# Causal attention and a gated MLP on one core: how VectorE adds 1e-9, what the planner takes TensorE to cost, and 66-column weight loads

## The chip, the cores and the metric

The kernel runs on one core of one Trainium2 chip. A core has TensorE (PE; its weight loads are listed as PEld), VectorE (DVE), ScalarE (ACT), GpSimd (POOL) and SyncE (SP), which here issues nearly all DMAs. The metric is the device time of one execution in microseconds (us), smaller is better.

## The reference

There are 4 batches of 12 heads, 448 positions, head size 64. Then comes an MLP on 1792 tokens of width 768 with a hidden width of 1536. All data is float32.

```python
scores = scale * np.matmul(q, k.transpose(0, 1, 3, 2))
scores = np.where(mask, -1000000000.0, scores)          # mask: above the diagonal
scores = scores - np.max(scores, axis=-1, keepdims=True)
attn = np.exp(scores)
attn = attn / (np.sum(attn, axis=-1, keepdims=True) + 1e-09)
x = attn @ v                                             # heads side by side: (1792, 768)
g = x @ w_gate
out = (g * (1 / (1 + np.exp(-g))) * (x @ w_val)) @ w_out
```

## The kernel before, in words

The work goes in four chunks, one for each batch. A *unit* is one head of one batch, 48 in all; numbers in names such as T24_2 or S22 begin with the unit's number. Heads are worked in pairs. While the MLP of chunk c runs on TensorE, the attention of chunk c+1 is mixed into it, a few matmuls at a time.

Precision: an operand of a matmul is split into a rounded high part and a low remainder (`xh`, `xl`; `hh`, `hl`; `ph`, `pl`; both halves of `whl`), and three products high x high, high x low, low x high are added (`mm3`, lines 871 to 876). The weights of the MLP are unpacked and split once, during chunk 0: a `wide` tile is loaded, ACT or POOL writes `top`, DVE builds `wraw` (L857), ACT or POOL rounds it into the high half of `whl` and DVE or POOL subtracts to get the low half (L333 or L336). The split is stored to DRAM, and later chunks load it back.

The attention of a unit, in the order of its stages: `score` (L505, 24 matmuls for a pair of heads, written "S"); `rowmax` (L553, DVE, four blocks: mask, scale, row minimum of the negated scores, an accumulator read behind each); `expo` (L565, ACT, writes the row's sum into `sums`); `recip` (L576 and L577, DVE: add 1e-9, then the reciprocal); normalising `p` (L609 on ACT, L613 on POOL, or DVE); `transp` and `transp0` (L699, L667: transposes of `p` into a bank "T"); an eviction of T into `ph` (ACT L311 or DVE L314), the remainder into `pl` or the low part of `ph` (DVE L333); `pv` (L741, seven matmuls into a bank "O").

From chunk 1 on there is one T bank, so a group of transposes starts only when the `ph` and the `pl` of the group before have been read out of it. A score needs four banks (two tags of two), so the score of the next pair waits for all eight rowmax blocks of the pair before.

`FEW` (line 51) is the number of columns that a weight load takes where 64 would do: the first block of a score (L504) and the `pl` matmuls (L740).

The order of the work is not written by hand: `Planner.run` (line 104) is a list scheduler. Every operation has the engines that could do it, each with a cost in us (`cost`, line 64; for TensorE also `TURN`, line 42, added where the kind of matmul changes: m for the MLP, s score, t transpose, o `pv`, v `pv` of chunk 0), and a due time. The planner picks operation by operation, by these numbers, on which engine and in which place it stands; the engines then run in that order, with semaphores. Its numbers change no instruction, only the order and the engine. `NR` (line 24) is the number of rows of `sums` and `rec` that units take in turn.

Of the kernel before, what the change touches and what calls it, by code (L numbers as in the profile page):

```python
# [8 lines left out]
F32 = mybir.dt.float32  # L9
# [6 lines left out]
ALU = mybir.AluOpType  # L16

P = 128
D = 64
# [1 line left out]
CUTS = [[0, 64, 192, 320, 448], [0, 64, 192, 320, 448], [0, 64, 192, 320, 448], [0, 64, 192, 320, 448]]  # L21
WID = [0, 64, 192, 320, 448]
CHUNKS = [[(0, 0, 448)], [(1, 0, 448)], [(2, 0, 448)], [(3, 0, 448)]]
NR = 8
SLOPE0 = 1.0
WLEAD = 1.2
XD = [-10.0, 3.0]
# [11 lines left out]
SHARED = 0.5  # L39
PVLATE = 0  # L40
LAT = {"PE": 0.29, "DVE": 0.2, "ACT": 0.23, "POOL": 0.2, "SP": 0.1}
TURN = {'ms': 0.19, 'sm': 0.19, 'mt': 0.0, 'tm': 0.0, 'ts': 0.19, 'st': 0.19, 'mv': 0.15, 'vm': 0.15, 'tv': 0.15, 'vt': 0.15, 'sv': 0.15, 'vs': 0.15, 'om': 0.055, 'os': 0.1, 'so': 0.19, 'ot': 0.03}
TS = 0.0
PF = 1.12
GF = 1.25
# [18 lines left out]
def cost(e, kind, n):  # L64
    if e == "ACT":
        return {"psum": 66, "sbuf": 110, "ptr": 190, "exp": 280, "tanh": 160}[kind] / 1e3 + n / 1200
    if e == "DVE":
        return 0.075 + n / {"one": 1920}.get(kind, 960)
    if e == "POOL":
        return {"one": 190, "ptr": 260, "two": 180}[kind] / 1e3 + n / {"two": 465.0}.get(kind, 1200.0)  # L70
    return {"r": max(n * 0.4475e-3 + 0.0025, 0.109), "n": n / 600, "t": n * 0.109 / 128}[kind] + 0.001


class Res:
# [154 lines left out]
def kernel(  # L229
# [8 lines left out]
    nc = tc.nc  # L238
# [5 lines left out]
    NKC = len(CUTS[0]) - 1  # L244
# [5 lines left out]
    cpool = ctx.enter_context(tc.tile_pool(name="cpool", bufs=1))  # L250
# [12 lines left out]
    masks = cpool.tile([P, P + maskX + P], F32, tag="masks", name="masks")  # L263
    back, mask = masks[:, : maskX + P], masks[:, P:]
    both = cpool.tile([P, D], F32, tag="both", name="both")
    all_sums = cpool.tile([P, NR, NKC], F32, tag="sums", name="sums")
    sums = [all_sums[:, i] for i in range(NR)]
    all_rec = cpool.tile([P, NR, NKC], F32, tag="rec", name="rec")
    rec = [all_rec[:, i] for i in range(NR)]
    xs = [cpool.tile([P, T], F32, tag=f"xs{i}", name=f"xs{i}") for i in range(KD)]  # L270
    xh = [cpool.tile([P, T], F32R, tag=f"xh{i}", name=f"xh{i}") for i in range(KD)]
# [9 lines left out]
    cpool.tile([P, 32], F32, tag="pad", name="pad")  # L281
    top = cpool.tile([P, WC], U32, tag="top", name="top")
    nc.vector.memset(top, 0)
    nc.vector.memset(all_sums, 1.0)
    make_identity(nc, ident)
    nc.gpsimd.memset(masks, 0.0)
    for m_, step, base in ((back, 1, 1 - P), (mask, -1, maskX)):
# [10 lines left out]
    def op(alts, due, deps=(), alloc=(), uses=(), extra=0.0):  # L298
        first = [heads[r.tag] for r in alloc if r.tag in heads]
        o = pl_.op(alts, due, list(deps) + first, alloc, uses, extra)  # L300
        o.soft = first
        o.port = bool(alts.pop("port", False))
        o.kb = alts.pop("kb", 0)
        o.kind = alts.pop("kind", "m")
        for r in alloc:
            heads[r.tag] = o
        return o
# [77 lines left out]
    st = [dict() for _ in range(NU)]  # L385
# [6 lines left out]
    def attention(u):  # L392
        U = units[u]
        c, b, h, N, KB = U.c, U.b, U.h, U.n, U.qb
        s = st[u]
# [4 lines left out]
        due = dues[u] = lambda stage: base + (SLOPE if c else SLOPE0) * stage  # L400
# [68 lines left out]
        if h % 2 == 0:  # L469
            if not U.ns:  # L470
                rQ, rK = Res("QS"), Res("KS")
                sp = []
                for nm, r_, src, ld, rr in (("Q", rQ, "q", lq, rq), ("K", rK, "k", lk, rk)):
                    def newsp(nm=nm):
                        s[nm] = buf([P, 2, S], F32R, nm + "S", nm + "S", f"{nm}S{u}")
                        return s[nm][:, 0]
                    x1 = op(copies("sbuf", N, newsp, lambda src=src: s[src + "w"]), due(0), [ld], [r_], [rr])
                    sp.append(op(binary(N, lambda nm=nm: s[nm][:, 1], lambda src=src: s[src + "w"],
                                        lambda nm=nm: raw(s[nm])[:, 0]), due(1), [x1], [], [r_, rr]))
            for gi_, sess in enumerate(FIRST if rest else SG if c == 0 else [sum(SG, [])]):  # L480
                tags = ["S", "X"] if c else ["SXM"[gi_]] if rest else ["MS"[gi_ == 0]]
                rSs = {(y, x): Res(tags[x]) for x in range(len(sess)) for y in (0, 1)}
                steps = sorted(sum(sess, []))

                def score(gi_=gi_, sess=sess, steps=steps, tags=tags):
                    passes = ((None, None),) if U.ns else ((0, 0), (0, 1), (1, 0))
                    for x, blks in enumerate(sess):
                        for y in (0, 1):
                            B_, off = bank(tags[x], f"S{u + y}_{gi_}_{x}"), 0
                            for i in blks:  # L490
                                q1_ = U.qi[i][1][1]
                                st[u + y][f"S{i}"] = B_[:, off : off + q1_]
                                off += q1_
                    for i in steps:
                        q0, q1_ = U.qi[i][1]
                        for z, (a, b_) in enumerate(passes):
                            for y in (0, 1):
                                half = slice(D * y, D * y + D)
                                Q = s["qw"][half] if U.ns else s["Q"][half, a]
                                K = s["kw"][half] if U.ns else s["K"][half, b_]  # L500
                                if U.joint and i == 0:
                                    nc.tensor.matmul(st[u]["S0"][half], Q[:, :D], K[:, :D] if y else K[:, S - D :], start=True, stop=True)
                                    continue
                                r = max(U.rows[i], FEW)  # L504
                                nc.tensor.matmul(st[u + y][f"S{i}"][:r], Q[:, q0 : q0 + r],  # L505
                                                 K[:, :q1_] if y else K[:, S - q1_ :], start=z == 0, stop=z == len(passes) - 1)
                ws = [U.qi[i][1][1] for i in steps]
                if U.ns:
                    so = op({"PE": (sum(cost("PE", "n", w) + 0.06 for w in ws) + TS, score), "kind": "s"}, due(2),
                            (rest if gi_ else some) or [lq, lk], list(rSs.values()), [rq, rk])  # L510
                else:
                    so = op({"PE": (sum(3 * cost("PE", "r", w) for w in ws) + TS, score), "kind": "s"}, due(2), sp,
                            list(rSs.values()), [rQ, rK])
                for x, blks in enumerate(sess):
                    for i in blks:
                        for y in (0, 1):
                            scored[u + y, i] = (so, rSs[y, x])
        for i, (q0, q1_) in U.own:
            r = U.rows[i]
# [17 lines left out]
            so, rS = scored[u, i]  # L537
# [34 lines left out]

        def recip():
            i0, i1 = U.own[0][0], U.own[-1][0] + 1
            sm, rc = sums[u % NR][:, i0:i1], rec[u % NR][:, i0:i1]
            nc.vector.tensor_scalar(rc, sm, 1.0e-9, None, ALU.add)  # L576
            nc.vector.reciprocal(rc, rc)  # L577
        rc = op({"DVE": (0.3, recip)}, due(5), exps, [], [rsum])

# [138 lines left out]
    def weigh(u):  # L718
# [6 lines left out]
        if not npv:  # L725
            rO, dps, use, dur = Res("O"), [], [], 0.0
            for g, o_, w, _, stk, d_, r_ in (blocks[j] for j in range(nj)):
                dps += [x for x in d_ if x not in dps]
                use += [r for r in r_ if r not in use]
                dur += (1 if stk else 2) * cost("PE", "r", w)  # L730

            todo = [(j, "ph") for j in (0, *range(2, nj))] + [(j, "pl") for j in range(nj - 1, 0, -1)] + [(1, "ph")]

            def pv():
                s["O"] = bank("O", f"O{u}")


                for x, (j, t) in enumerate(todo):
                    g, o_, w, _, stk, _, _ = blocks[j]
                    m = FEW if t == "pl" else 2 * D  # L740
                    nc.tensor.matmul(s["O"][:m, U.base(j) - U.qa : N], s["VS"][:, j, :m], s[f"{t}{g}"][:, o_ : o_ + w],  # L741
                                     start=x == 0, stop=x == len(todo) - 1)
            last = op({"PE": (dur, pv), "kind": "o"}, due(10), dps, [rO], use)
            rx, rt = Res(f"xs{h}"), Res("tmp")

            def newt():
                s["tmp"] = buf([D, S], F32, "tmp", "tmp", f"tmp{u}")[:, :N]
                return s["tmp"]
            t1 = op(copies("psum", N, newt, lambda: s["O"][D:P, :N], engines="AD"), due(11), [last], [rt], [rO])
            o = op(binary(N, lambda: xs[k][D * (h % 2) : D * (h % 2) + D, :N], lambda: s["O"][0:D, :N],  # L750
                          lambda: s["tmp"], ALU.add, engines="D"), due(12), [t1] + prevx, [rx], [rO, rt])
            xs_ops.setdefault((c, k), []).append(o)
            xs_res.setdefault((c, k), []).append(rx)
            return
# [261 lines left out]
```

## Time and profile before

| | us |
|---|---|
| median of 3 runs | 683.66 (683.42 to 683.88) |
| the profiled execution | 684.65 |
| its span, first to last instruction | 682.9 |

TensorE's records cover 98% of the span at full granted clock (0.999). The end of a matmul is modelled and matmuls overlap, so what a matmul takes of the stream is read from the start of one to the start of the next. The rows of the profile in the section below are named by their group.

### The profile page before, as it was taken

How to read it: one execution, taken by the hardware profiler on the slowest of the kernel's cores; microseconds unless marked ns; L12 is line 12 of the kernel's file. 1: busy time of each engine (PE TensorE's matmuls, PEld its weight loads, DVE VectorE, ACT ScalarE, POOL GpSimd, SP SyncE). 2: the span in 40 equal slices, each digit the busy share in tenths (PEclk: the TensorE clock that was granted, in tenths of full speed). 3: DMA queues.
4: the chain of work that ended last, by engine and by line, in shares of the span. 5: the costliest groups of instructions: out<-in, count | busy, mean ns of one | idle time of the engine just before them, and what ended most of it. 6: DMA issues, size and time to landing. Idle time of an engine off the chain costs nothing.

```text
span 682.9 us, 10861 instructions
## 1 busy us (share of the span) xinstructions
PE 671.8 (98%) x3898; PEld 598.9 (88%) x3898; DVE 356.7 (52%) x881; ACT 347.8 (51%) x864; POOL 193.7 (28%) x238
## 2 busy tenths in 40 slices
PE   9999999999999999999999999999999999999998
PEld 6567898899888999999999989999999999999997
DVE  5777889898788464355633346545444222222100
ACT  6998688687798363245634336346345211111000
POOL 3766455556162130031322214134232000000000
PEclk9999999999999999999999999999999999999999
DMA  8878899999988865556667665554555675676771
GB/s 293 277 260 308 303 352 390 321 374 314 347 309 324 320 202 201 191 176 215 202 223 239 201 230 189 200 186 139 186 198 164 216 224 213 223 229 212 226 251 41
DMA packets 40118, 165.08 MB, mean 242 GB/s; under 512 B 4480, under 2 KB 13952, under 8 KB 40064
## 3 DMA queue, kind: packets, MB, share of 16 engines
q1 hardware_dynamic: 39904, 164.28, 70.6%
q8 instruction: 31, 0.51, 0.3%
q14 instruction: 23, 0.19, 0.1%
q10 hardware_dynamic: 160, 0.10, 0.1%
HBM read 130.55 MB, written 33.82 MB: 241 GB/s over the span
## 4 chain that ended last, share of the span: by engine, by line
PE 81%; ACT 11%; DVE 6%; issue 1%; POOL 0%; ACTq 0%; DVEq 0%
PE M L874 15%; PE M L875 15%; PE M L876 15%; PE MO L874 8%; PE MO L875 8%; PE MO L876 7%; PE S L505 4%; PE O L741 4%; ACT p L565 4%; PE T L699 3%; ACT p L609 2%; ACT ph L311 1%; ACT top L311 1%; DVE wraw L857 1%; PE T L667 1%
## 5 line engine op out<-in xcount | busy, mean ns | idle before, releaser
L874 PE MATMUL M<-xh,whl 128*128 128x448 f32 x576 | 215.0, 373 | 0.0
L875 PE MATMUL M<-xl,whl 128*128 128x448 f32 x576 | 209.4, 364 | 0.0
L876 PE MATMUL M<-xh,whl 128*128 128x448 f32 x576 | 209.1, 363 | 0.0
L874 PEld LDWEIGHTS M<-xh,whl 128*128 128x128 f32 x576 | 108.2, 188 | 8.5 <-issue 1.7
L876 PEld LDWEIGHTS M<-xh,whl 128*128 128x128 f32 x576 | 108.1, 188 | 7.7
L875 PEld LDWEIGHTS M<-xl,whl 128*128 128x128 f32 x576 | 108.4, 188 | 6.8 <-DVE xl L333 0.3
L874 PE MATMUL MO<-hh,whl 128*128 128x448 f32 x288 | 107.2, 372 | 0.0
L876 PE MATMUL MO<-hh,whl 128*128 128x448 f32 x288 | 104.6, 363 | 0.6 <-DVE whl L333 0.6
L875 PE MATMUL MO<-hl,whl 128*128 128x448 f32 x288 | 104.7, 364 | 0.0
L565 ACT ACTIVATE p<-p,m 128x192 f32<-128x192 f32 (+3 forms) x180 | 91.1, 509 | 3.4 <-DVE m L553 3.3
L311 ACT ACTIVATE ph<-T 128x384 fp32r<-128x384 f32 (+3 forms) x116 | 57.8, 504 | 56.5 <-PE T L667 34.4
L553 DVE CUSTOM_DVE_ANT_0 p<-S,masks 128x192 f32<-128x192 f32 (+3 forms) x180 | 68.3, 426 | 21.4 <-PE S L505 20.2
L311 ACT ACTIVATE hh<-t 128x448 fp32r<-128x448 f32 x40 | 23.1, 577 | 82.0 <-DVE t L917 82.0
L609 ACT ACTIVATE p<-p,rec 128x192 f32<-128x192 f32 (+3 forms) x130 | 58.8, 502 | 9.3 <-DVE rec L577 9.0
L911 DVE SCALAR_TENSOR_TENSOR t<-t,M 128x448 f32<-128x448 f32 x48 | 29.7, 619 | 57.2 <-ACT t L907 56.8
L876 PEld LDWEIGHTS MO<-hh,whl 128*128 128x128 f32 x288 | 54.0, 188 | 4.7 <-DVE whl L333 1.0
L874 PEld LDWEIGHTS MO<-hh,whl 128*128 128x128 f32 x288 | 54.1, 188 | 4.5 <-issue 1.2
L875 PEld LDWEIGHTS MO<-hl,whl 128*128 128x128 f32 x288 | 54.2, 188 | 3.6 <-DVE hl L333 0.3
L917 DVE TENSOR_TENSOR t<-t,M 128x448 f32<-128x448 f32 x48 | 29.6, 618 | 51.0 <-PE M L876 50.6
L907 ACT ACTIVATE t<-M 128x448 f32<-128x448 f32 x48 | 26.0, 542 | 57.5 <-PE M L876 56.9
L333 DVE TENSOR_TENSOR pl<-T,ph 128x384 fp32r<-128x384 f32 x72 | 39.6, 550 | 22.6 <-ACT ph L311 22.3
L699 PE MATMUL T<-ident,p 128*128 128x128 f32 x288 | 46.8, 276 | 3.3 <-DVE pl L333 3.0
(80 smaller groups left out, 822.7 us busy)
## 6 DMA issues: line engine op xcount, KB each, us to landing
whl<-ws SPq DMA_DIRECT2D x108, 768.0 KB, 4.4
wide<-in_w_dram SPq DMA_DIRECT2D x36, 768.0 KB, 6.8
ws<-whl SPq DMA_DIRECT2D x36, 768.0 KB, 7.5
vraw<-in_v_dram SPq DMA_DIRECT2D x24, 256.0 KB, 4.3
out_dram<-osb SPq DMA_DIRECT2D x24, 224.0 KB, 4.7
qraw<-in_q_dram SPq DMA_DIRECT2D x23, 224.0 KB, 4.6
kraw<-in_k_dram SPq DMA_DIRECT2D x23, 224.0 KB, 4.6
qraw<-in_q_dram SPq DMA_DIRECT2D x1, 128.0 KB, 2.5
```

Source lines behind the costliest of these rows:

```text
L311: nc.scalar.activation(out(), in_(), AF.Copy, scale=scale)
L333: r["DVE"] = (cost("DVE", "two", n), lambda: nc.vector.tensor_tensor(out(), a(), b(), alu))
L505: nc.tensor.matmul(st[u + y][f"S{i}"][:r], Q[:, q0 : q0 + r], K[:, :q1_] if y else K[:, S - q1_ :], start=z == 0, stop=z == len(passes) - 1)
L553: nc.vector.tensor_tensor_reduce(p[:r], s[f"S{i}"][:r], mask[:r, maskX - q0 : maskX - q0 + q1_] if h % 2 else back[:r, P - min(q1_, P) : P ...
L565: nc.scalar.activation(p[:r], p[:r], AF.Exp, bias=peak(i)[:r], scale=-1.0, accum_out=sums[u % NR][:r, i : i + 1],)
L609: nc.scalar.activation(p[:r], p[:r], AF.Copy, scale=rec[u % NR][:r, i : i + 1])
L699: nc.tensor.transpose(pt[:, o_ + q0 - bs : o_ + q0 - bs + r], s[f"p{i}"][:r, k0 : k0 + P], ident[:r, :r])
L874: nc.tensor.matmul(out[:, :n], a[:, w], xhi, start=first, stop=False)
L875: nc.tensor.matmul(out[:, :n], a[:, w], xlo, start=False, stop=False)
L876: nc.tensor.matmul(out[:, :n], l[:, w], xhi, start=False, stop=last)
L911: nc.vector.scalar_tensor_tensor(t, t, 1.0, ps[c, f, 0][:, :N], ALU.add, ALU.mult)
L917: nc.vector.tensor_tensor(t, t, ps[c, f, 1][:, :N], ALU.mult)
```

## The change: a sum over pairs, other numbers for the planner, 66 columns

`sums` gets one more row, which is set to 1e-9 once. The first step of `recip` is now a `tensor_reduce` with add over an axis of two: the unit's row and that constant row, reached by a stride. The units take 7 rows in turn instead of 8. The planner's costs change: of turns on TensorE, of a score's 64-wide block (0.062 us a matmul instead of 0.109), and of `pv` (0.001 us more or less a matmul, by width). `FEW` is 66.

```diff
-NR = 8
+NR = 7
...
-TURN = {'ms': 0.19, 'sm': 0.19, 'mt': 0.0, ... 'om': 0.055, 'os': 0.1, 'so': 0.19, 'ot': 0.03}
+TURN = {'ms': 0.15, 'sm': 0.17, 'mt': 0.0, ... 'om': 0.0, 'os': 0.1, 'so': 0.16, 'ot': 0.0}
...
-FEW = 72
+FEW = 66
...
-    return {"r": max(n * 0.4475e-3 + 0.0025, 0.109), "n": n / 600, ...
+    return {"r": max(n * 0.4475e-3 + 0.0025, 0.109), "f": n * 0.4475e-3 + 0.0045, "n": n / 600, ...
...
-    all_sums = cpool.tile([P, NR, NKC], F32, tag="sums", name="sums")
+    all_sums = cpool.tile([P, NR + 1, NKC], F32, tag="sums", name="sums")
...
-    nc.vector.memset(all_sums, 1.0)
+    nc.vector.memset(all_sums[:, :NR], 1.0)
+    nc.vector.memset(all_sums[:, NR], 1.0e-9)
...
-  so = op({"PE": (sum(3 * cost("PE", "r", w) for w in ws) + TS, score), "kind": "s"}, due(2), sp,
+  so = op({"PE": (sum(3 * (0.062 if w == D else cost("PE", "r", w)) for w in ws) + TS, score), "kind": "s"}, due(2), sp,
...
-            sm, rc = sums[u % NR][:, i0:i1], rec[u % NR][:, i0:i1]
-            nc.vector.tensor_scalar(rc, sm, 1.0e-9, None, ALU.add)
+
+            sm, rc = all_sums[:, u % NR :: NR - u % NR, i0:i1], rec[u % NR][:, i0:i1]
+            nc.vector.tensor_reduce(rc, sm.rearrange("p a c -> p c a"), mybir.AxisListType.X, ALU.add)
             nc.vector.reciprocal(rc, rc)
...
-                dur += (1 if stk else 2) * cost("PE", "r", w)
+                dur += (1 if stk else 2) * cost("PE", "f", w)
```

In the changed kernel, lines 285 to 575 stand one lower than before, and later ones two.

Where the order moves, first VectorE behind the first transposes of unit 36 in chunk 2 (rec and sums are shared by all units; T36_1 is a bank of transposes, ph and pl its two evictions). Before:

```order
L577 RECIPROCAL rec_70<-rec_70 128x4
L917 TENSOR_TENSOR t2_0_4627<-t2_0_4627,M2_1_4621 128x448
L314 TENSOR_SCALAR ph36_1_4682<-T36_1_4673 128x384
L576 TENSOR_SCALAR rec_70<-sums_69 128x4
L577 RECIPROCAL rec_70<-rec_70 128x4
L333 TENSOR_TENSOR pl36_1_4690<-T36_1_4673,ph36_1_4682 128x384
L314 TENSOR_SCALAR ph36_2_4706<-T36_2_4697 128x384
```

And the same place now:

```order
L579 RECIPROCAL rec_70<-rec_70 128x4
L919 TENSOR_TENSOR t2_0_4626<-t2_0_4626,M2_1_4622 128x448
L315 TENSOR_SCALAR ph36_1_4683<-T36_1_4674 128x384
L578 TENSOR_REDUCE rec_70<-sums_69 128x4
L579 RECIPROCAL rec_70<-rec_70 128x4
L334 TENSOR_TENSOR pl36_1_4691<-T36_1_4674,ph36_1_4683 128x384
L315 TENSOR_SCALAR ph36_2_4707<-T36_2_4698 128x384
```

Here nothing moved: the reduction stands where the addition stood, between the two evictions.

Second, TensorE at the end of chunk 0, ahead of the score of units 24 and 25 (MO0 is an output bank of the MLP of chunk 0, whl a weight tile, S24 and S25 the score's banks). Before:

```order
L876 MATMUL MO0_3_2560<-hh4_93,whl30_2458 128x448
L874 MATMUL MO0_3_2560<-hh5_94,whl30_2458 128x448
L875 MATMUL MO0_3_2560<-hl5_106,whl30_2458 128x448
L876 MATMUL MO0_3_2560<-hh5_94,whl30_2458 128x448
L699 MATMUL T22_1_2601<-ident_66,p22_1_2529 128x128
L699 MATMUL T22_1_2601<-ident_66,p22_2_2531 128x128
L699 MATMUL T22_1_2601<-ident_66,p22_3_2535 128x128
L505 MATMUL S24_0_0_2606<-KS24_2525,QS24_2523 72x64
L505 MATMUL S25_0_0_2607<-KS24_2525,QS24_2523 72x64
```

And now:

```order
L877 MATMUL MO0_2_2393<-hl11_112,whl29_2441 128x448
L878 MATMUL MO0_2_2393<-hh11_100,whl29_2441 128x448
L743 MATMUL O21_2542<-ph21_0_2419,VS21_2238 128x448
L743 MATMUL O21_2542<-ph21_2_2522,VS21_2238 128x256
L743 MATMUL O21_2542<-ph21_2_2522,VS21_2238 128x128
L743 MATMUL O21_2542<-pl21_2_2533,VS21_2238 66x128
L743 MATMUL O21_2542<-pl21_2_2533,VS21_2238 66x256
L743 MATMUL O21_2542<-pl21_1_2503,VS21_2238 66x384
L743 MATMUL O21_2542<-ph21_1_2491,VS21_2238 128x384
L506 MATMUL S24_0_0_2570<-KS24_2493,QS24_2482 66x64
L506 MATMUL S25_0_0_2571<-KS24_2493,QS24_2482 66x64
```

The score of units 24 and 25 moved ahead of the transposes T22_1 and of 27 matmuls of the MLP: between it and the score of units 22 and 23 there now stand two groups of three transposes, 18 matmuls of the MLP and one `pv`; before there stood one `pv`, 27 matmuls and one group of three.

Third, TensorE where chunk 1's MLP begins (M1_0 is its first bank; T24_2 and T25_0 both use the one T bank). Before:

```order
L874 MATMUL M1_0_3007<-xh5_82,whl36_2838 128x448
L875 MATMUL M1_0_3007<-xl5_88,whl36_2838 128x448
L876 MATMUL M1_0_3007<-xh5_82,whl36_2838 128x448
L699 MATMUL T24_2_3038<-ident_66,p24_2_2668 128x128
L699 MATMUL T24_2_3038<-ident_66,p24_3_2675 128x128 x2
L874 MATMUL M1_1_3046<-xh0_77,whl37_2852 128x448
L875 MATMUL M1_1_3046<-xl0_83,whl37_2852 128x448
```

And now:

```order
L506 MATMUL S29_0_0_2976<-KS28_2832,QS28_2830 128x448
L701 MATMUL T24_2_3008<-ident_66,p24_2_2637 128x128
L701 MATMUL T24_2_3008<-ident_66,p24_3_2649 128x128 x2
L669 MATMUL T25_0_3024<-ident_66,p24_0_2413 128x128
L669 MATMUL T25_0_3024<-ident_66,p24_1_2628 128x128
L669 MATMUL T25_0_3024<-ident_66,p24_2_2637 128x128
L669 MATMUL T25_0_3024<-ident_66,p24_3_2649 128x128
L876 MATMUL M1_0_3029<-xh0_77,whl36_2901 128x448
```

T25_0 now stands right behind T24_2, with no matmul of another kind between; before, 54 matmuls of the MLP stood between them.

## Rows read from the trace of the kernel before

**Rows 1.** Page, part 1: engine, busy us (share of the span) xinstructions.

```profile
PE 671.8 (98%) x3898; PEld 598.9 (88%) x3898; DVE 356.7 (52%) x881; ACT 347.8 (51%) x864; POOL 193.7 (28%) x238
```

**Rows 2.** Waits of PE: line <- what ended them: us in total, times, longest.

```profile
PE T L699 <- DVE pl L333: 3.0, 4, 1.4
PE O L741 <- DVE ph L333: 1.2, 2, 1.0
...
PE MO L876 <- DVE whl L333: 0.6, 1, 0.6
```

**Rows 3.** Line L576: count, ns min/median/max, first and last start us, forms.

```profile
L576 DVE TENSOR_SCALAR rec<-sums x48: 151/170/1625, 9.3 to 527.8; 128x4 f32<-128x4 f32 x42, 128x3 f32<-128x3 f32 x6
```

**Rows 4.** Line L577, same columns.

```profile
L577 DVE RECIPROCAL rec<-rec x48: 175/178/179, 9.5 to 528.0; 128x4 f32<-128x4 f32 x42, 128x3 f32<-128x3 f32 x6
```

**Rows 5.** Timeline of DVE, 394 to 398: start us, us, line, operation [idle before].

```profile
394.65 0.56 DVE L314 TENSOR_SCALAR ph<-T 128x384 fp32r<-128x384 f32 x1 [0.31 <-PE T L699]
395.12 1.14 DVE L576 TENSOR_SCALAR rec<-sums 128x4 f32<-128x4 f32 x1
...
396.39 0.53 DVE L333 TENSOR_TENSOR pl<-T,ph 128x384 fp32r<-128x384 f32 x1
```

**Rows 6.** Timeline of POOL, 394 to 398.

```profile
395.08 1.16 POOL L336 TENSOR_TENSOR hl<-t,hh 128x448 fp32r<-128x448 f32 x1
```

**Rows 7.** Timeline of PE, 394 to 398.

```profile
394.12 0.49 PE L699 MATMUL T<-ident,p 128*128 128x128 f32 x3
394.37 0.45 PE L874 MATMUL M<-xh,whl 128*128 128x448 f32 x1
...
397.06 0.52 PE L699 MATMUL T<-ident,p 128*128 128x128 f32 x3 [0.64 <-DVE pl L333]
```

**Rows 8.** Timeline of PE, at 69.

```profile
69.20 0.52 PE L699 MATMUL T<-ident,p 128*128 128x128 f32 x3 [1.40 <-DVE pl L333]
```

**Rows 9.** Timeline of DVE, at 67.

```profile
66.78 1.62 DVE L576 TENSOR_SCALAR rec<-sums 128x4 f32<-128x4 f32 x1 [0.18 <-ACT p L565]
...
68.53 0.53 DVE L333 TENSOR_TENSOR pl<-T,ph 128x384 fp32r<-128x384 f32 x1
```

**Rows 10.** Timeline of POOL, at 67.

```profile
66.55 1.82 POOL L336 TENSOR_TENSOR whl<-wraw,whl 128x768 fp32r<-128x768 f32 x1
```

**Rows 11.** Lines of PEld, by form: names, shapes xcount | busy us, mean ns.

```profile
L741 PEld LDWEIGHTS O<-pl,VS 128*72 128x72 f32 x108 | 9.8, 144 | 0.0
```

**Rows 12.** Page, part 5: line L874's loads.

```profile
L874 PEld LDWEIGHTS M<-xh,whl 128*128 128x128 f32 x576 | 108.2, 188 | 8.5 <-issue 1.7
```

**Rows 13.** Timeline of PE, 300 to 304: a score amid the MLP.

```profile
300.98 0.36 PE L876 MATMUL M<-xh,whl 128*128 128x448 f32 x1
301.27 1.85 PE L505 MATMUL S<-KS,QS 64*72 64x64 f32 x24
303.05 0.47 PE L874 MATMUL M<-xh,whl 128*128 128x448 f32 x1
303.36 0.37 PE L875 MATMUL M<-xl,whl 128*128 128x448 f32 x1
```

**Rows 14.** Timeline of PE, 186 to 200: scores of units 22 and 24.

```profile
188.36 1.84 PE L505 MATMUL S<-KS,QS 64*72 64x64 f32 x24
...
196.97 1.84 PE L505 MATMUL S<-KS,QS 64*72 64x64 f32 x24
```

**Rows 15.** Timeline of DVE, 109 to 112: four rowmax blocks.

```profile
109.45 0.20 DVE L553 CUSTOM_DVE_ANT_0 p<-S,masks 64x64 f32<-64x64 f32 x1
...
110.83 0.07 DVE L553 DVE_READ_ACCUMULATOR2_ANT m<- 128x1 f32 x1
```

**Rows 16.** Lines of DVE, by form.

```profile
L857 DVE SCALAR_TENSOR_TENSOR wraw<-wide,top 128x768 uint32<-128x768 uint32 x36 | 39.5, 1098 | 6.3 <-ACT top L311 5.9
L333 DVE TENSOR_TENSOR whl<-wraw,whl 128x768 fp32r<-128x768 f32 x28 | 31.6, 1129 | 0.9 <-ACT whl L311 0.9
```

**Rows 17.** Windows: stretch, its us, then busy (x) of PE, PEld, DVE, ACT, POOL.

```profile
55.60:182.00 126.40, 123.95 (x735) 111.59 (x734) 109.47 (x218) 100.56 (x225) 67.63 (x60) 1.00 0.95 339
```

More of the change, by code (lines that the diff above doesn't have):

```diff
@@ L41 @@
 LAT = {"PE": 0.29, "DVE": 0.2, "ACT": 0.23, "POOL": 0.2, "SP": 0.1}
-TURN = {'ms': 0.19, 'sm': 0.19, 'mt': 0.0, 'tm': 0.0, 'ts': 0.19, 'st': 0.19, 'mv': 0.15, 'vm': 0.15, 'tv': 0.15, 'vt': 0.15, 'sv': 0.15, 'vs': 0.15, 'om': 0.055, 'os': 0.1, 'so': 0.19, 'ot': 0.03}
+TURN = {'ms': 0.15, 'sm': 0.17, 'mt': 0.0, 'tm': 0.0, 'ts': 0.15, 'st': 0.17, 'mv': 0.15, 'vm': 0.15, 'tv': 0.15, 'vt': 0.15, 'sv': 0.15, 'vs': 0.15, 'om': 0.0, 'os': 0.1, 'so': 0.16, 'ot': 0.0}
 TS = 0.0
@@ L70, in cost @@
         return {"one": 190, "ptr": 260, "two": 180}[kind] / 1e3 + n / {"two": 465.0}.get(kind, 1200.0)
-    return {"r": max(n * 0.4475e-3 + 0.0025, 0.109), "n": n / 600, "t": n * 0.109 / 128}[kind] + 0.001
+    return {"r": max(n * 0.4475e-3 + 0.0025, 0.109), "f": n * 0.4475e-3 + 0.0045, "n": n / 600, "t": n * 0.109 / 128}[kind] + 0.001
 class Res:
@@ L265 @@
     both = cpool.tile([P, D], F32, tag="both", name="both")
-    all_sums = cpool.tile([P, NR, NKC], F32, tag="sums", name="sums")
+    all_sums = cpool.tile([P, NR + 1, NKC], F32, tag="sums", name="sums")
     sums = [all_sums[:, i] for i in range(NR)]
-    all_rec = cpool.tile([P, NR, NKC], F32, tag="rec", name="rec")
+    all_rec = cpool.tile([P, NR + 1, NKC], F32, tag="rec", name="rec")
     rec = [all_rec[:, i] for i in range(NR)]
```

## Prediction, made before the changed kernel had run

> **What bounds the kernel now.** I read the page first: TensorE is covered for 98% of the span, and no other engine for more than 52% [rows 1]. So the end is set by how long TensorE's stream is and by the holes in it. Next the waits of TensorE alone: only a few microseconds are idle, and nearly all of it is ended by VectorE: 3.0 us where transposes wait for `pl` to be read out of the bank, 1.2 where `pv` waits for the low part of `ph`, 0.6 for a split weight [rows 2]. At full clock the stream itself can shrink only by cheaper turns and loads; everything else that the change can do is to make these holes smaller or larger. A change of 1.4 us (0.2% of 683.66) is about what a measurement can tell from nothing, and all the holes together are some 6 us.
>
> Then I asked what is late behind the holes. At 397.06 TensorE's second group of transposes waits 0.64 us for a `pl` [rows 7]. VectorE's queue ahead of that `pl` holds the 1e-9 addition of another unit: it begins at 395.12 and takes 1.14 us, and the `pl` starts at 396.39 [rows 5]. The addition's median is 0.170 us and its longest 1.625, for the same 4 numbers a partition [rows 3]. At 395.08 GpSimd began a subtraction of 1.16 us [rows 6]: it ends at 396.24, and the addition at 396.26. At 66.78 the same: the addition takes 1.62 us [rows 9], inside a GpSimd subtraction from 66.55 to 68.37 [rows 10], the `pl` starts at 68.53, and TensorE, idle for 1.40 us, starts at 69.20 [rows 8]. So VectorE's addition waits for GpSimd's running instruction to end, and twice that wait reaches TensorE. The reciprocal right behind has never taken more than 0.179 us [rows 4].
>
> By the Trainium skill (SBUF — State Buffer, "Who interferes with whom"), GpSimd shares a port pair with VectorE under an exclusive lock, `tensor_scalar` can need that pair, and `tensor_reduce` on this chip never contends. The trace agrees on the first two, the ends lying 0.02 us apart; no run so far shows the third.
>
> **The change, part by part.** All terms are set against the profiled execution (684.65, its span 682.9) and then moved to the median of the runs, which is 0.99 below it.
>
> *The addition becomes a reduction over pairs.* Still 48, one for each unit, in the same step of the same queue. Its own price: 8 numbers a partition read instead of 4. No row has a small reduction; below stands the shortest addition, 0.151, above it the longest, 1.625 [rows 3]; the nearest is the reciprocal, 0.178, also four results from a strided row and never held up [rows 4]. I take 0.18. If it isn't held by GpSimd, the two waits above end: at unit 36 the order around it is unchanged, so the `pl` comes 1.14 - 0.18 = 0.96 us sooner, and the 0.64 of idle time goes [rows 5, 7]. At 69.20 the hole of 1.40 us goes likewise, for the `pl` comes 1.44 sooner [rows 8, 9]. Together -2.0. Ends: 0 (it is held as before) and -3.0, all of the transposes' wait [rows 2].
>
> The skill has a rule against this: a `tensor_reduce` is the slowest VectorE operation and should be restructured away on a hot path (VectorE: DVE Perf Modes, "Rules for kernel authors"). The reciprocal's row says that at this size the fixed part is nearly all. By that rule the 48 reductions would cost a little more each on an engine that is 52% busy; by the row, nothing. The sum goes by the row.
>
> One more memset, and 7 rows in turn instead of 8 (a unit then waits for the normalisation of the unit 7 before it, long done): nothing.
>
> *66 columns.* A load of 72 columns takes 144 ns [rows 11], one of 128 takes 188 [rows 12]: 0.79 ns a column, 4.7 ns for six. There are 108 such loads in scores and 108 in `pv`. If each is in the way, 216 x 4.7 = 1.0 us; if the matmuls cover them, 0. Only the first block of a score (64 columns a matmul) and the 128-wide matmuls of `pv` are short enough to let a load show, about half: -0.5.
>
> *The order: turns.* From the order, TensorE changes kind 292 times before and 287 times now, and five scores, not two, now lead straight into transposes. A score amid the MLP costs 0.29 us up to its start, and 0.31 from the next matmul to the second, where a step of the MLP is 0.20 [rows 13]; so a turn is worth 0.1 us, and five to three of them -0.3. Ends 0 and -0.6.
>
> *The order: the end of chunk 0.* Here the new order puts work closer to what it waits for. Four places:
>
> (a) T25_0 right behind T24_2 in the one bank. At 394.12 a group of three transposes starts; the eviction starts at 394.65 and takes 0.56 [rows 5], `pl` then 0.53, and from its end to TensorE's start it is 0.14 (68.53 + 0.53 to 69.20) [rows 8, 9]: ready at 395.88, while TensorE went on at 394.37 [rows 7]. What was covered by 54 matmuls is now bare: +1.5.
>
> (b) The score of units 24 and 25. In the order before, the two scores start 8.61 us apart [rows 14]. Nine MLP matmuls fewer (-1.8) and one group of transposes more (+0.3) make 7.1. In that time VectorE must do, from the end of the first score (1.8): eight rowmax blocks (four take 1.45 to the last read's end [rows 15], so 2.9), two evictions of `ph` and two `pl` (2.2 [rows 5]), one `wraw` (1.10 [rows 16]), one reduction and reciprocal (0.36): 8.4, less some overlap and plus whatever it was behind with. I take +1.5, between 0.5 and 2.5.
>
> (c) `pv` of unit 22 six matmuls (1.2 us) behind T23_0, while VectorE has a weight subtraction of 1.13 [rows 16], a 448-wide one and the low part of `ph` in front of it: +1.1, between 0 and 2.
>
> (d) The MLP's first matmuls behind the score wait for a weight subtraction that VectorE does after the rowmax blocks: +0.5, between 0 and 1.
>
> Sum +4.6. In the same stretch the order before had 0.6 (the weight) [rows 2] and, of the 3.0 and the 1.2, what lies behind the holes at 69 and 397: 3.0 - 1.40 - 0.64 = 1.0 and 1.2 - 1.0 = 0.2. Up to 1.5 goes there, so +3.1 net. Ends: +0.5 and +5.
>
> *The order: the rest.* Before, 9 matmuls (1.8 us) stood between two groups of transposes nearly everywhere; now it is 12 at one of two such places. That gives the eviction and `pl` 0.6 us more. But 20 evictions of `ph` moved from ScalarE to VectorE (42 instead of 22 by the order), 0.56 us each [rows 5], 11 us of VectorE work in all. I take -0.8 for chunks 0 to 3 outside the places above, between -1.5 and +2.
>
> DMA: the queue issues the same 280 transfers; none ends a wait of TensorE before [rows 2], so nothing.
>
> Sum: -2.0 - 0.5 - 0.3 + 3.1 - 0.8 = -0.5. 684.65 - 0.5 = 684.15 for such an execution, 683.2 for the median.
>
> **The rivals.**
>
> *Faster: the end of chunk 0 isn't as tight as I count.* VectorE is 109.5 us busy in the 126.4 us from 55.6 to 182 [rows 17]; the held additions are gone, so it may come to the end of the chunk ahead of time, and (b), (c) and (d) shrink to 0.5 in all. (a) and this 0.5 stand against 1.5 of old holes, +0.5: -2.0 - 0.5 - 0.3 + 0.5 - 0.8 = -3.1, that is 680.6. For it speaks that three of four places have a low end near nothing; against it that the work in front of them (weights, rowmax) cannot be put off.
>
> *Slower: VectorE becomes the bound of chunk 0.* It is at 0.87 of that stretch [rows 17]. Roughly half of the 11 us moved onto it falls in chunk 0, +5.5, against some 3 us of held additions that go. If it gets over 0.9, it has no idle time left to catch up after a wait for ScalarE, every late `pl` or low `ph` reaches TensorE, and 2.5 us more are lost: 685.7. It decides from the point where `pl` is late in 55.6 to 182 more often than before.
>
> *The reduction is held by GpSimd just the same.* Then the -2.0 falls out: 685.2. The never-held reciprocal speaks against it.
>
> **How the numbers follow.** The sum, no change that can be told: 0.38, own range 682.3 to 685.0. Faster, about 680.6: 0.35. Slower: VectorE the bound 0.21, the reduction held 0.06, together 0.27. The range that holds 8 in 10 reaches into both rivals, 680.3 to 686.0. Likeliest 683.2.
>
> **What would show it.** Right: the longest reduction is under 0.3 us; at unit 36 the second group of transposes has no idle time before it; in TensorE's waits T25_0 has about 1.5 us, ended by `pl` or by the eviction; the score of units 24 and 25 waits for rowmax; the 66-column loads take about 139 ns. Wrong: reductions as long as a GpSimd instruction; no wait at T25_0; or a total over 686 with TensorE waiting on VectorE throughout 55 to 182 (the order as a whole is then worse, not its end), or under 680 with the end of chunk 0 free of waits.

## The result, and the profile after

The changed kernel took 689.38 us (median of 5, 689.26 to 690.66), the kernel before 683.88 beside it (683.42 to 685.04): 1.0083 times as long, 95% interval 1.0069 to 1.0098. It is slower by 5.5 us, outside the predicted range, and by none of the rivals' mechanisms. The profiled execution took 689.36, its span is 687.6.

The page of the changed kernel, part 1, columns as in [rows 1]:

```profile
PE 675.3 (98%) x3898; PEld 598.0 (87%) x3898; DVE 357.2 (52%) x902; ACT 338.6 (49%) x844; POOL 186.4 (27%) x238
```

TensorE is still covered for 98% of the span, but for 3.5 us more than in [rows 1], with the same 3898 matmuls. So part of the loss lies inside its stream and shows in no wait. The waits of the changed kernel's TensorE, as [rows 2]:

```profile
PE MO L878 <- DVE whl L334: 1.6, 2, 1.3
PE T L669 <- DVE pl L334: 1.3, 1, 1.3
PE T L701 <- DVE pl L334: 1.1, 3, 0.6
PE S L506 <- DVE m L554: 0.9, 1, 0.9
PE T L669 <- POOL p L615: 0.7, 1, 0.7
PE T L701 <- DVE m L554: 0.7, 1, 0.7
```

Of the 3.0 us behind `pl` at the line of the transposes 1.1 are left, and other waits stand beside them: a split weight, the one bare pair of transpose groups (L669 behind `pl` is T25_0), the rowmax blocks (`m`), and once a normalisation of `p` on GpSimd.

The additions of the changed kernel by line (count, ns min/median/max), against [rows 3, 4]:

```profile
L578 DVE TENSOR_REDUCE rec<-sums x48: 140/156/165, 9.4 to 528.5; 128x4 f32<-128x8 f32 x42, 128x3 f32<-128x6 f32 x6
L579 DVE RECIPROCAL rec<-rec x48: 175/178/180, 9.6 to 528.7; 128x4 f32<-128x4 f32 x42, 128x3 f32<-128x3 f32 x6
```

No reduction is held: 165 ns is the longest, where an addition took up to 1625.

Now the stream itself. The prediction took one step of it, 0.20 us [rows 13], as given. The trace shows the step best where nothing but the MLP's matmuls is left. The timeline of the kernel before, TensorE at 600 us (start us, us):

```profile
600.09 0.36 PE L874 MATMUL M<-xh,whl 128*128 128x448 f32 x1
600.29 0.36 PE L875 MATMUL M<-xl,whl 128*128 128x448 f32 x1
...
601.29 0.36 PE L874 MATMUL M<-xh,whl 128*128 128x448 f32 x1
```

The same in the changed kernel:

```profile
600.11 0.37 PE L878 MATMUL M<-xh,whl 128*128 128x448 f32 x1
600.32 0.37 PE L876 MATMUL M<-xh,whl 128*128 128x448 f32 x1
...
601.14 0.37 PE L877 MATMUL M<-xl,whl 128*128 128x448 f32 x1
```

Six steps take 1.20 us before, a step of 200 ns. After, five take 1.03: 206 or 207 ns. The matmul, its tiles and its shape are the same. The windows of TensorE alone (stretch, its us, busy and matmuls in it, granted clock, DMA share, GB/s) make it countable, first of before, then of the changed kernel:

```profile
550.00:600.00 50.00, 50.00 (x252) 1.00 0.66 224
600.00:650.00 50.00, 50.00 (x252) 1.00 0.69 223
```

```profile
550.00:600.00 50.00, 50.00 (x244) 1.00 0.66 212
600.00:650.00 50.00, 50.00 (x244) 1.00 0.63 211
```

Both are busy for the whole stretch at a granted clock of 1.00, with 252 matmuls in 50 us and with 244. From about 549 us on, some 650 follow one another: 650 x 6.67 ns = 4.3 us that no view of waits or busy shares shows. A step count over the whole trace (differences of starts of neighbouring MLP matmuls) finds 200 and 206.7 as two steady values; a run of MLP matmuls mostly keeps one of them until the next group of another kind. Behind all 17 `pv` with loads of 72 columns that the MLP follows at once it is 200 in the kernel before. In the changed one, with 66 columns, it is 206.7 behind 15 of 19, and 200 behind the other four, which all stand before 210 us.

### The profile page after: what moved, and what is told of

Read it like the earlier page. It is cut to its first block, busy times and chain, and to the rows that moved or that the text cites. A ratio compares the mean times of both kernels' runs of the same rounds, so it can differ in the third digit from the quotient of the medians.

```text
span 687.6 us, 10870 instructions
## 1 busy us (share of the span) xinstructions
PE 675.3 (98%) x3898; PEld 598.0 (87%) x3898; DVE 357.2 (52%) x902; ACT 338.6 (49%) x844; POOL 186.4 (27%) x238
## 4 chain that ended last, share of the span: by engine, by line
PE 82%; ACT 9%; DVE 7%; issue 2%; DMA 0%; POOL 0%; ACTq 0%; DVEq 0%
PE M L876 15%; PE M L877 15%; PE M L878 15%; PE MO L876 7%; PE MO L877 7%; PE MO L878 7%; PE S L506 5%; PE O L743 4%; PE T L701 3%; ACT p L566 3%; ACT p L611 2%; DVE wraw L859 2%; DVE whl L334 2%; PE O L774 1%; PE T L669 1%
## 5 line engine op out<-in xcount | busy, mean ns | idle before, releaser
L312 ACT ACTIVATE ph<-T 128x384 fp32r<-128x384 f32 (+3 forms) x96 | 47.9, 508 | 64.6 <-PE T L701 32.7
L312 ACT ACTIVATE hh<-t 128x448 fp32r<-128x448 f32 x44 | 25.3, 575 | 84.9 <-DVE t L919 84.9
L611 ACT ACTIVATE p<-p,rec 64x64 f32<-64x64 f32 (+3 forms) x122 | 54.7, 504 | 5.7 <-DVE rec L579 5.6
L615 POOL TENSOR_SCALAR p<-p,rec 128x448 f32<-128x448 f32 (+3 forms) x58 | 36.4, 634 | 63.0 <-DVE rec L579 46.6
```

What stands on the lines that cost most here:

```text
L312: nc.scalar.activation(out(), in_(), AF.Copy, scale=scale)
L611: nc.scalar.activation(p[:r], p[:r], AF.Copy, scale=rec[u % NR][:r, i : i + 1])
L615: nc.gpsimd.tensor_scalar(p[:r], p[:r], rec[u % NR][:r, i : i + 1], 0.0, ALU.mult, ALU.add)
```

## The experiments

The four first ones take the change apart. None of the edits but that of the planner's numbers moves an instruction.

**66 columns alone** (kernel before):

```
-FEW = 72
+FEW = 66
```

Expected: 

> The kernel before with loads of 66 instead of 72 columns and nothing else; every engine's order stays. Theory A (the columns set TensorE's step: an MLP matmul behind a pv takes 207 ns after 66-column loads, 200 after 72): the last stretch of some 650 matmuls is at 207, +4.4 us, with the shorter runs behind other pv some +6 us, 690 in all. Theory B (the new order, with VectorE the bound of chunk 0, made it slower): no more than the shorter loads, 683.4.

Measured: 689.25 us (688.40 to 690.32), 1.0076 times before, 1.0063 to 1.0088. The windows of TensorE:

```profile
550.00:600.00 50.00, 50.00 (x244) 1.00 0.63 217
600.00:650.00 50.00, 50.00 (x244) 1.00 0.63 215
```

The slow step came with the columns alone, with order and addition as before: +5.3 us, as much as the whole change. As the order is the same, the two traces can be laid side by side, matmul by matmul: from 56 us on this kernel falls back by 5.2 us, 4.3 of them in the last stretch.

**The reduction alone** (kernel before, 72 columns, its order; 7 rows in turn and the row of 1e-9 as in the change):

```
-            nc.vector.tensor_scalar(rc, sm, 1.0e-9, None, ALU.add)
+            sm, rc = all_sums[:, u % NR :: NR - u % NR, i0:i1], rec[u % NR][:, i0:i1]
+            nc.vector.tensor_reduce(rc, sm.rearrange("p a c -> p c a"), mybir.AxisListType.X, ALU.add)
```

Expected: 

> The kernel before with the sum over pairs alone (and 7 rows); the order stays. If the reduction isn't held by GpSimd: longest under 0.2 us, the idle time of 1.40 us at 69 and of 0.64 us at 397 gone, -2 us, 681.9. If a lateness is only handed on: 683.9. Theory A and B both say nothing on it; A expects the step behind a pv to stay at 200 ns.

Measured: 678.50 us (677.93 to 678.82), 0.9918 times before, 0.9905 to 0.9931: -5.5 us, far more than expected. The places of [rows 5 to 10] in this kernel: VectorE ahead of unit 36's second group, then TensorE at both places.

```profile
389.44 0.56 DVE L315 TENSOR_SCALAR ph<-T 128x384 fp32r<-128x384 f32 x1 [0.31 <-PE T L700]
389.91 0.15 DVE L577 TENSOR_REDUCE rec<-sums 128x4 f32<-128x8 f32 x1
390.09 0.18 DVE L578 RECIPROCAL rec<-rec 128x4 f32<-128x4 f32 x1
390.19 0.52 DVE L334 TENSOR_TENSOR pl<-T,ph 128x384 fp32r<-128x384 f32 x1
```

```profile
65.32 0.41 PE L700 MATMUL T<-ident,p 128*128 128x128 f32 x2
...
391.05 0.38 PE L700 MATMUL T<-ident,p 128*128 128x128 f32 x2
```

What took 1.14 us takes 0.15, and neither transpose has idle time before it. More of the gain stands in TensorE's waits:

```profile
PE O L742 <- DVE ph L334: 0.8, 1, 0.8
...
PE T L700 <- DVE pl L334: 0.5, 1, 0.5
...
PE MO L877 <- DVE whl L334: 0.3, 1, 0.3
```

Against [rows 2], `pl` went from 3.0 to 0.5, `ph` from 1.2 to 0.8, the weight from 0.6 to 0.3: 3.2 us, and TensorE loses some 0.16 more at each restart that falls away (idle time counts from a modelled end 0.36 us after a start, and a step is 0.20). The spans differ by more, 6.7, but some 2 of these are no work of the reduction: in the two traces the first transposes begin at 12.45 and 10.23 us, and with 66 columns alone, where the addition is the old one, at 10.37. Laid side by side, matmul by matmul, the two traces differ by 2.4 us at 56 us (1.4 with 66 columns alone), and 4.3 come behind it, above all 1.5 at 69 us, 0.3 at 204, 0.4 at 214, 0.2 at 218, 0.8 at 397 and 0.4 at 503. How much of the 2.4 is the reduction's isn't shown.

The trace of before has more held additions than these two: 13 of the 48 took 0.28 to 1.63 us, 9.1 us above the median in all, and each ended 22 to 30 ns behind the end of an instruction of GpSimd.

**The order alone** (kernel before with the new numbers of the planner, which give the changed kernel's order; 72 columns, old addition):

```
-TURN = {'ms': 0.19, 'sm': 0.19, ...
+TURN = {'ms': 0.15, 'sm': 0.17, ...
...
+ ... 3 * (0.062 if w == D else cost("PE", "r", w)) ...
...
+ ... cost("PE", "f", w)
```

Expected: 

> The kernel before with the planner's new numbers alone: the order of the changed kernel, 72 columns, the addition as before. Theory A: the last stretch stays at 200 ns; the order itself costs between 0 and +2 us: 684 to 686. Theory B: nearly the whole loss, 689.

Measured: 688.87 us (687.49 to 689.52), 1.0065 times before, 1.0052 to 1.0078: +4.9 us. Some of it is TensorE's clock, as the next run shows.

**The changed kernel with 72 columns:**

```
-FEW = 66
+FEW = 72
```

Expected: 

> The changed kernel with 72 columns again. Theory A: the step behind a pv is 200 ns again, 5.5 to 6.5 us less than the changed kernel: 683 to 684. Theory B: as the changed kernel, 689.5.

Measured: 684.77 us (682.69 to 687.18, 12 runs), 1.0012 times before, 1.0001 to 1.0023. So on the new order 66 columns cost 4.6 us and the reduction gives 4.1 (688.87 to 684.77). The three parts in this order: +4.9 - 4.1 + 4.6 = +5.4, the measured loss. In this trace TensorE's clock fell behind the waits at 205.7 and 207.0 us. Its timeline, then its windows:

```profile
205.70 0.47 PE L878 MATMUL MO<-hh,whl 128*128 128x448 f32 x1 [1.28 <-DVE whl L334]
...
208.49 0.57 PE L876 MATMUL MO<-hh,whl 128*128 128x448 f32 x1
208.86 0.57 PE L877 MATMUL MO<-hl,whl 128*128 128x448 f32 x1
```

```profile
208.20:211.20 3.00, 3.00 (x10) 0.54 0.59 199
211.20:214.00 2.80, 2.80 (x33) 1.00 0.30 121
```

A step is 370 ns at a granted 0.54, about the lower of the two levels (1.2 GHz), and 1.00 is back afterwards. Seven such steps cost 1.2 us, the `pv` ahead of them another 0.5. The changed kernel's own trace has the same wait and no such fall. The trace of the order alone has the fall too, behind a wait of 1.69 us at 207.63:

```profile
210.40:212.40 2.00, 2.00 (x7) 0.50 0.66 245
```

Each run's mean granted clock is on record; 3 us at 0.54 in a span of 684.7 make 0.998. The six of these 12 runs at 0.998 have a median of 685.4 us, the six at 0.999 or 1.000 one of 683.9, so a lower clock goes with some 1.5 us of the wide spread; what parts the rest (682.7 to 684.7) stays open. Of the five runs of the order alone, two are at 0.997 (689.4 and 689.5) and three above it (687.5 to 688.9); of the changed kernel none is below 0.999. By the medians of the runs at the higher clock (688.2 and 683.9) the order costs +4.2, the reduction gives 4.3 and the columns cost 5.5.

**72 columns in the last unit's `pv` alone** (changed kernel, three loads of the program):

```
-                    m = FEW if t == "pl" else 2 * D
+                    m = (72 if u == NU - 1 else FEW) if t == "pl" else 2 * D
```

Expected: 

> The changed kernel with 72 instead of 66 columns in the low loads of the last unit's pv alone (three matmuls of the program); order, reduction and every other load as in the changed kernel. Theory A (the width of the three short loads in the last group of another kind sets the step of the 650 MLP matmuls behind it, 200.0 or 206.7 ns): the stretch from 549 us on goes back to 200 ns, 650 x 6.67 ns = 4.3 us less, 685.0 us; the rest of the trace keeps its 206.7 ns behind every other pv. Rival (the step depends on something that all 216 loads share, for instance the program's size or the time of the loads in sum): 689.4 as the changed kernel, the tail at 206.7.

Measured: 686.24 us (684.85 to 687.19, 10 runs), 1.0025 times before, 1.0015 to 1.0036: 3.1 us less than the changed kernel by the medians, 4.5 by the profiled spans (683.1 against 687.6). The windows:

```profile
550.00:600.00 50.00, 50.00 (x252) 1.00 0.67 222
600.00:650.00 50.00, 50.00 (x252) 1.00 0.67 222
```

Three loads, 18 columns in all, set the pace of 650 matmuls behind them. The medians give back less than the 4.3; the runs lie at 685 and at 686.3, and what parts them stays open.

**66 columns in the scores alone, and in `pv` alone** (both on the kernel with the reduction, 678.50):

```
-                                r = max(U.rows[i], FEW)
+                                r = max(U.rows[i], 66)
```

Expected: 

> The kernel before with the reduction (678.5 us measured), and 66 columns in the first blocks of the scores alone; pv keeps its 72. Theory A: scores do not set the step, for behind a score both kernels showed the same steps; 108 loads a few ns shorter at most, 678.0 to 678.6. Rival (the scores' loads matter as well): up to 683.

```
-                    m = FEW if t == "pl" else 2 * D
+                    m = 66 if t == "pl" else 2 * D
```

Expected: 

> The kernel before with the reduction (678.5 us measured), and 66 columns in the low loads of pv alone; the scores keep 72. Theory A: all of the loss of the 66 columns is here: every run of MLP matmuls behind a pv steps by 206.7 ns, the last 650 too, 4.3 to 5.3 us more: 682.8 to 683.8. Rival (the loss needs the scores' 66 too, or comes from them): about 678.5.

Measured: 677.74 us (677.17 to 678.73), 0.9907 times before, 0.9891 to 0.9924; and 684.07 (682.84 to 684.87), 0.9998, 0.9988 to 1.0008. All of the loss is in `pv`. The first is the fastest kernel of this study, 6.1 us under before; its lead over 72 columns, 0.8, lies inside the spread.

One part of theory A missed. With 66 in `pv` alone the step is 206.7 behind all ten `pv` that themselves follow MLP matmuls, the last one among them, but behind six of the seven that follow a score it goes to 200 after some four steps. With 66 in the scores too (66 columns alone, above) it stays at 206.7 behind six of these seven, and so it does behind unit 43 in the last scan below, where the reduction is in too. So behind a score the score's loads bear on the step as well.

**70, 128 and 68 columns** (the kernel with the reduction; 70 in scores and `pv`, then 128 and 68 in `pv` with 66 in the scores; columns beyond the first 64 add products of two low parts to the sum):

```
+FEW = 70
...
+                    m = 2 * D
...
+                    m = 68 if t == "pl" else 2 * D
```

Expected: 

> The kernel before with the reduction (678.5 us measured), and 70 columns in the short loads of scores and pv. Theory A1 (what counts is whether the columns are a multiple of four: 72 is, 66 and 70 are not): the steps behind pv are 206.7 ns, 682.8 to 683.8. Theory A2 (what counts is that the load is long enough, and 70 is next to 72): 200 ns, 678.3 to 678.6.

> The kernel with the reduction, 66 columns in the scores (677.74 us measured) and full loads of 128 columns in the low matmuls of pv. If only the width of the load sets the step, it stays at 200 ns or takes a third value. A load is 44 ns longer than one of 72, 108 of them, at most 4.7 us if no matmul covers them: 677.7 to 682 at 200 ns; 673 at a step of 193; 682 to 686 at 206.7.

> The kernel with the reduction, 66 columns in the scores (677.74 us measured) and 68 in the low loads of pv. The step behind a pv was 200 ns at 70 and 72 and 206.7 at 66, so 68 tells on which side of it the border lies: 677.3 to 678.5 at 200 ns, 682 to 684 at 206.7.

Measured: 679.14 us (678.94 to 680.94), 0.9925, 0.9908 to 0.9943; 686.73 (685.64 to 687.92), 1.0043, 1.0029 to 1.0058; 678.11 (677.07 to 678.67), 0.9916, 0.9896 to 0.9936. In the stretch from 550 to 600 us of the 128-column kernel:

```profile
550.00:600.00 50.00, 50.00 (x244) 1.00 0.63 213
```

In this last stretch the step is 200 ns with 68, 70 and 72 columns, with 66 and with 128 it is 206.7. A multiple of four isn't the rule (70), nor is one border in width. The total with 128 lies 0.7 above the range expected for 206.7.

The trace with 70 columns shows that the width doesn't decide alone: the step is 200 behind all ten `pv` that follow MLP matmuls, and 206.7 behind all seven that follow a score. First behind one of the ten, then behind one of the seven:

```profile
378.26 0.36 PE L876 MATMUL MO<-hl,whl 128*128 128x448 f32 x1
...
379.46 0.36 PE L876 MATMUL MO<-hl,whl 128*128 128x448 f32 x1
...
414.66 0.37 PE L875 MATMUL M<-xh,whl 128*128 128x448 f32 x1
...
415.90 0.37 PE L875 MATMUL M<-xh,whl 128*128 128x448 f32 x1
```

Six steps take 1.20 us, and then 1.24.

**A scan of widths in one trace.** 16 `pv` that the MLP follows at once get each its own width, the others 72; the step is read behind each:

```
+PVW = {13: 64, 15: 65, 17: 67, 19: 69, 21: 71, 23: 73, 25: 74, 27: 76, 29: 78, 31: 80, 33: 84, 35: 88, 37: 96, 39: 104, 41: 112, 43: 120}
...
+                    m = PVW.get(u, FEW) if t == "pl" else 2 * D
```

Expected: 

> The kernel with the reduction and 66 columns in the scores; the low loads of pv have 64, 65, 67, 69, 71, 73, 74, 76, 78, 80, 84, 88, 96, 104, 112 and 120 columns in units 13, 15, ... to 43, and 72 in all others. Read from the trace: the step of the MLP's matmuls right behind each of these pv. Theory P (the time at which the last load ends against the matmuls' pace decides, and a pace of 16 cycles locks in): both steps alternate as the width grows, several stretches of each. Theory W (a window of widths round 70 is good): 200 ns from 67 to some width above 72, 206.7 on both sides. The last 650 matmuls at 200; the total 677 to 680.

Measured: 678.84 us in a single run (before 683.83). Two neighbours of the scan, TensorE behind 112 and behind 120 columns:

```profile
463.20 0.37 PE L876 MATMUL M<-xh,whl 128*128 128x448 f32 x1
...
464.85 0.37 PE L878 MATMUL M<-xh,whl 128*128 128x448 f32 x1
...
490.09 0.37 PE L876 MATMUL M<-xh,whl 128*128 128x448 f32 x1
490.30 0.36 PE L877 MATMUL M<-xl,whl 128*128 128x448 f32 x1
...
491.90 0.36 PE L876 MATMUL MO<-hh,whl 128*128 128x448 f32 x1
```

Eight steps take 1.65 us behind 112 columns (206), and nine 1.81 behind 120, the first of 0.21 and then 200 each. In all: 206.7 ns behind 65, 71, 73, 78, 88 and 112 columns, 200 behind 64, 67, 69, 74, 76, 80, 104 and 120, and 200 after some four longer steps behind 84 and 96. The two alternate, as theory P expected; the window of widths (theory W) is out. That the end of the last load decides, as P has it, isn't shown by this. And each width was read at one place: seven of them (67, 69, 71, 96, 104, 112, 120) behind a `pv` that follows a score, the others behind one that follows the MLP. As 70 columns gave both steps by place, this list holds for its places and not for the widths as such.

**One or two of the three loads at a time** (same kernel, widths of the first, second and third low load by unit):

```
+PVW = {13: (66, 72, 72), 15: (72, 66, 72), 17: (72, 72, 66), 19: (66, 66, 72), 21: (66, 72, 66), 23: (72, 66, 66), ...
```

Expected: 

> The same kernel with 72 columns in all pv but these: 66 in the first, the second, the third of the three low loads alone (units 13, 15, 17, and again 37, 39, 41), in two of them (19, 21, 23), in all (43), and 128 in one or two of them (25 to 35). Theory P1 (the last short load decides): 206.7 ns behind 17, 41, 21, 23 and 43, 200 behind 13, 15, 19, 37 and 39. Theory P2 (the sum of the three decides): the same step wherever the one load stands. The total 677 to 680.

Measured: 680.38 us in a single run. One load of 66 gave 206.7 ns, whichever of the three it was and in both units tried (13, 15, 17 and 37, 39, 41); two of 66 gave 200 (19, 21, 23; behind 19 and 23 after four steps), three again 206.7 (43). So the last load doesn't decide alone (P1 falls). With 128 in one of the three it was 200 (25, 27, 29; behind 25 after four steps). With 128 in two of them it was 200 (31, and 35 after four steps) and 206.7 (33). These three have the same sum, 328 columns, and all follow MLP matmuls, so the plain sum doesn't decide either (P2 falls). What lines the pace up stays open.

**Two other orders** (the kernel with the reduction and one of the planner's new numbers: the prices of the turns, then the price of a `pv`):

Expected: 

> The kernel before with the reduction (678.5 us measured) and the eight changed prices of the turns alone, 72 columns: a third order. At the end of chunk 0 T25_0 stands right behind T24_2, as in the changed kernel. Theory (the order's loss is the end of chunk 0: the bare pair of groups and VectorE behind it): 1.3 us of idle time at T25_0 and some 2 us more between 187 and 235 us, 681 to 683.5. Rival (the loss of the order lies in the whole of chunks 0 to 3, or needs all of the numbers): 678.0 to 680.

> The kernel before with the reduction (678.5 us measured) and the changed price of a pv alone, 72 columns: a fourth order, with 54 MLP matmuls between T24_2 and T25_0, as before. Theory (the order's loss is the end of chunk 0): nothing of the 1.3 us at T25_0, 677.5 to 679.5. Rival (any move of the order away from the one before costs): 681 to 683.

Measured: 679.20 us (678.48 to 680.76), 0.9937, 0.9915 to 0.9959; and 678.70 (677.85 to 679.68), 0.9922, 0.9900 to 0.9944. The first order has the bare pair of groups too, and its trace shows the price:

```profile
223.24 0.66 PE L668 MATMUL T<-ident,p 128*128 128x128 f32 x4 [1.38 <-DVE pl L334]
```

Yet the kernel loses 0.7 us against the old order, not 2.5 to 5: here the theory of the end of chunk 0 missed. The bare pair costs its 1.4 and little else; the weights and scores behind VectorE, which cost the rest in the changed kernel, aren't late in this one (TensorE is busy for all 19.00 us from 187 to 206). The second order, without the bare pair, came out inside the range of its theory, so a move of the order alone needn't cost.

## Why the prediction was wrong, step by step

*The step that failed most is "66 columns": -0.5 between 0 and -1.0, measured +5.3 alone, and +4.6 on the new order.* The loads did become shorter. With 66 columns alone a `pv` behind a score takes 1022 ns from its first start to the MLP's first instead of 1039, one behind MLP matmuls 913 as before. The mean of the loads fell from 144 ns [rows 11] to 137:

```profile
L743 PEld LDWEIGHTS O<-pl,VS 128*66 128x66 f32 x108 | 9.2, 137 | 0.2 <-DVE pl L334 0.2
```

The bounds took for granted that a shorter load can only help or do nothing. What the runs showed instead: the loads of a `pv` bear on the pace of the matmuls behind it, and three of them, 66 columns wide, slow the last 650 from 200 to 206.7 ns. In the scores alone the shorter loads gave 0.8 us, near the term and inside the spread. Steps of 206 and 207 ns stood in the trace of before (some 200 of them over the first 550 us, none in the last stretch), but the prediction read one "step of the MLP" of 0.20 [rows 13] and asked no further.

*"The addition becomes a reduction"* was right in its mechanism: nothing held, and both places free. Its size was off: -2.0, low end -3.0; measured -5.5, and -4.1 on the new order. The term counted only two holes with a held addition straight in front. A third, 0.28 us at 502.81 behind an addition of 0.77 us, was in the trace, so the prediction's "twice that wait reaches TensorE" was an undercount. With 13 additions held, all of the queue behind each was late, and in the places above so were the weight, the `ph` and the other `pl` that TensorE waited for. VectorE's busy time fell by 8 us in the kernel with the reduction alone (356.7 to 348.6 up to 670 us). The Trainium skill's rule that a `tensor_reduce` never contends on this chip (SBUF — State Buffer, "Who interferes with whom") now agrees with rows: 165 ns at most. The Trainium skill's rule against reductions on a hot path (VectorE: DVE Perf Modes, "Rules for kernel authors") doesn't bear here: the median is 156 ns, 14 less than the addition's.

*"The end of chunk 0"* came out in its sum, +4.6 gross, and the changed kernel's timeline of TensorE has the places in order, from the score of units 24 and 25 to T25_0:

```profile
192.04 1.82 PE L506 MATMUL S<-KS,QS 64*66 64x64 f32 x23 [0.92 <-DVE m L554]
...
195.09 0.47 PE L878 MATMUL MO<-hh,whl 128*128 128x448 f32 x1 [0.34 <-DVE whl L334]
...
227.89 0.66 PE L669 MATMUL T<-ident,p 128*128 128x128 f32 x4 [1.32 <-DVE pl L334]
```

(a) 1.5 expected, 1.32 measured. (b) 1.5, and 0.92. (c) 1.1, and 0.22 (the low `ph` at 205.97). (d) 0.5, and 0.34 + 1.27: the second weight came at 204.66, where VectorE had, among others, eight rowmax blocks (195.24 to 199.89) and a `wraw` of 1.44 ahead of it. Together 4.1. The four waits are the ones named, but that the sum fits is partly luck: (c) came far below its term and (d) as far above. Of the 1.5 of old holes set against it the reduction took half as well, so the two terms counted that half twice.

*"The rest of the order", -0.8, and the turns, -0.3,* failed: the order alone cost +4.9 (+4.2 by the runs at the higher clock), not the +2.0 of the three terms. No run parts the turns from the rest. The windows from 112 to 206 us (columns as in [rows 17]) show where, first of the kernel with the reduction in the old order:

```profile
112.00:187.00 75.00, 74.92 (x449) 67.53 (x449) 62.71 (x119) 57.42 (x125) 35.51 (x34) 1.00 0.95 340
187.00:206.00 19.00, 18.71 (x111) 16.80 (x110) 15.69 (x48) 18.95 (x55) 11.63 (x11) 1.00 0.88 314
```

and of the changed kernel:

```profile
112.00:187.00 75.00, 73.86 (x441) 66.75 (x440) 62.95 (x119) 55.63 (x120) 30.76 (x29) 1.00 0.91 329
187.00:206.00 19.00, 16.01 (x99) 13.06 (x97) 16.87 (x54) 18.23 (x53) 11.85 (x13) 1.00 0.91 307
```

TensorE is idle for 0.08 and 1.14 us in the first stretch, for 0.29 and 2.99 in the second (which are places (b) to (d) and one late `pl`). The 12 matmuls between groups did not help: in the first stretch `pl` is late at 146 and 171 us, and ScalarE's `t` at 157.

*The rivals.* "Faster" had the end of chunk 0 loose: it wasn't. "VectorE becomes the bound of chunk 0" had as its condition over 0.9 of 55.6 to 182. The windows of the changed kernel, against [rows 17]:

```profile
55.60:182.00 126.40, 124.49 (x732) 112.99 (x729) 109.20 (x226) 99.21 (x221) 57.74 (x56) 1.00 0.95 350
```

That is 0.86, as before, so over this stretch VectorE is late by its order and not by its load; only in the 19 us of the second stretch is it busier, 16.87 against 15.69. "Held just the same" fell at once.

*The signs.* Every sign named for being right came true: the longest reduction of 0.165 us, no idle time ahead of unit 36's second group, 1.32 us at T25_0, the score of units 24 and 25 behind rowmax, loads of 137 ns. The total still missed by 6.2 us, for no sign was set on the step of the stream.

## What to carry to other kernels

Where one kind of matmul repeats some hundred times at a busy share of 1.00, count its steps in a window before and after; a busy share hides a slower pace. A load made shorter is not free, nor is a longer one: read the step of the stream that follows. An instruction that another engine can hold costs more than the holes right behind it: add up what it makes late in its own queue.

## What the runs showed of the hardware

The same matmul of 448 columns, with its load of 128, repeats at 200.0 or at 206.7 ns, at a granted clock of 1.00 in both cases, and stays with one of them for 650 steps. The loads ahead of the stream bear on which it is: 72 columns instead of 66 in the three short loads of the last `pv` brought the 650 steps from 206.7 to 200. The width alone doesn't settle it. In the last stretch it was 200 behind 68, 70 and 72 columns and 206.7 behind 66 and 128, but in one trace 70 columns gave 200 behind a `pv` that follows the MLP and 206.7 behind one that follows a score, and 66 columns gave 200 behind four `pv` of the changed kernel. What decides stays open.

The Trainium skill gives N / 2.4 GHz + 2.5 ns for the gap of a single matmul at full clock (TensorE: Matmul & The Clock Gate, "Back-to-back issue gap"): 189 ns for 448 columns, as an estimate. The steps measured here are longer by 11 and by 18 ns. The same section says that in a stream of loads and matmuls both set the spacing, and a pace that changes with the loads ahead agrees with that.

An addition of 128x4 numbers on VectorE ended 22 to 30 ns behind an instruction of GpSimd in each of the 13 cases of 48 in which it took over 0.25 us; the reduction of 128x8 numbers took at most 0.165 us in the changed kernel's 48.
